# Sliding-window attention and gated feed-forward on one core: a reordered opening, six V buffers, rotating PSUM banks, last tiles in four banks

## The chip, the core and the metric

The kernel runs on one NeuronCore of a Trainium2 chip. The metric is the device time of one execution in microseconds (us). TensorE is called PE below, its weight load PEld, VectorE DVE, ScalarE ACT, GpSimd POOL, SyncE SP.

## The reference

Eight batches, eight heads, 576 positions, head size 64. Each position attends to itself and the 63 before it. The result, 4608 tokens of 512 numbers, goes through a gated feed-forward layer of width 1536.

```python
scores = q @ k.T / sqrt(64); mask = (rel >= 0) & (rel < 64)
x = softmax(scores, mask) @ v                  # then (4608, 512)
out = (silu(x @ w_gate) * (x @ w_val)) @ w_out # w: 512x1536, 512x1536, 1536x512
```

## The kernel before

Tokens are cut into 36 *chunks* of 128 and 9 *blocks* of 512 (four chunks). For each chunk `n` there are four steps on PE, each ended by copies on DVE or ACT: `T(n)` transposes K and Q, `Sx(n, half)` makes scores, `AV(n, half)` multiplies by V, and `X(n)` transposes the result into `xT`, the input of the feed-forward layer. For each block `c` there are 12 *feature slices* `F(c, f)`, two groups of four matmuls and then tanh on ACT and two DVE operations, and four *output tiles* `O(c, u)` of 12 matmuls. While block `c` is computed, the attention of the next four chunks is interleaved. PE writes its results into eight *banks* of a buffer named PSUM, from which DVE and ACT copy them; by the recorded order a bank is written again only when it has been emptied.

Each operation is recorded with the tiles that it reads and writes; each engine then runs its operations in the recorded order, and waits follow from reads and writes. Loads are issued by POOL, in the recorded order as well, and convert f32 to bf16 on the way. The window of a chunk reaches into the chunk before, so V is needed a second time, shifted by 64 rows: `vb[n]` holds the upper half of chunk `n-1` and the lower half of chunk `n`, copied within the core by DMAs that SP issues.

```python
NQ = 4; NV = 4; NZ = 3                          # buffers of q/k, v, transposed q
self.gb = ps[0:4]; self.ob = ps[4]; self.ab = ps[5:8]   # PSUM banks: F, O, attention

def load(self, n, which):
    ...                                         # POOL: q, k or v of chunk n, by HBM segments
    if which == "v":
        hi = [("va", i, 0), ("va", i, 1), ("va", i)]
        g.op("sp", ... dma_start(vb[64:128], va[0:64]), reads=hi, writes=[("vb", i, 1)], dma=True)
        if n + 1 < NCH:
            i2 = (n + 1) % self.NV              # n = 3: i2 = 0, the buffer of chunk 0
            g.op("sp", ... dma_start(vb2[0:64], va[64:128]), reads=hi, writes=[("vb", i2, 0)], dma=True)

def build(self):
    ...                                         # loads of chunks 0 to 3, weight slices 0 to 3
    self.T(0); self.Sx(0, 0); self.T(1); self.Sx(0, 1)
    for n in range(0, 4):
        self.AV(n, 0)
        self.Sx(n + 1, 0) if n < 3 else None
        self.AV(n, 1)
        self.Sx(n + 1, 1) if n < 3 else None
        self.X(n)
        if n < 2: self.T(n + 2)
    for w in late_w: self.load_w(*w)            # slices 4 to 11, 512 columns a piece
    more(4)                                     # q, k, v of chunk 4
    self.load_wo(0, 6); self.load_wo(6, 12)     # w_out
    more(5)                                     # q, k, v of chunk 5
    self.T(4); self.F(0, 0); self.Sx(4, 0); self.Sx(4, 1)
    for c in range(NFC):
        for u in range(4):
            n = 4 * c + u + 4
            more(n + 2)
            ...                                 # F(c, 3u); AV(n, 0); [T(5) if n == 4]; Sx(n+1, 0)
            ...                                 # F(c, 3u+1); AV(n, 1); Sx(n+1, 1); O(c-1, u)
            ...                                 # X(n); F(c, 3u+2); T(n+2)
    for u in range(4): self.O(NFC - 1, u)       # the last four tiles, all in bank 4
```

The softmax here doesn't subtract the row's maximum and nothing guards it: scores larger than these inputs give would overflow.

## Time and profile before

| | before |
|---|---|
| time, median of 4 runs | 404.03 us |
| span of the profiled run | 403.1 us |
| first AV | 23.5 us |
| first feature slice | 40.2 us |
| second block starts | 85.97 us |
| last four output tiles start | 386.58 us |

The page cuts the span into 40 slices of about 10 us. A digit is the busy share in tenths; PEclk is the granted PE clock, DMA the mean busy share of the 16 DMA engines.

```profile
PE   1156498789999999999999999999999999999975
PEclk9999879989999999999999999999999999999999
DMA  9999996667777888787887777777777310010012
```

PE is full from the tenth slice on. Before that it is not, and for the first six slices the DMA engines are full instead: the loss lies in the opening, and at the very end.

The windows view gives busy us (and instructions) of PE, PEld, DVE, ACT and POOL in a stretch, then granted clock, DMA share (the summed time of the packets over that of 16 engines, which can pass 1) and GB/s. The third line is the steady part, from the second block to the last tiles; the fourth is the end.

```profile
40.00:50.00 10.00, 4.32 (x36) 2.59 (x36) 4.36 (x10) 2.90 (x6) 1.75 (x2) 0.90 1.91 183
50.00:60.00 10.00, 9.41 (x62) 4.97 (x62) 5.63 (x12) 3.79 (x7) 2.62 (x3) 0.76 1.69 154
...
85.97:386.58 300.61, 296.33 (x2099) 159.12 (x2137) 209.47 (x441) 121.46 (x209) 65.83 (x79) 1.00 0.60 73
386.58:403.10 16.52, 10.83 (x47) 4.37 (x48) 0.00 (x0) 2.39 (x4) 0.00 (x0) 1.00 0.16 63
```

The steady part is 98.6% PE (296.33 of 300.61 us), so nothing but the first 86 us and the last 16.5 us can give much. The chain that ended last (start, length, what) shows where the opening waits:

```profile
12.84 10.66 issue
23.50 0.22 PE ps L355
...
29.16 18.28 DMA kn<-in_k_dram
```

Two large pieces stand there: 10.66 us of "issue", which means that the profile shows no releaser, ahead of the first AV (L355), and a DMA of 18.28 us, the K of chunk 5, ahead of `T(5)` (L307). The timeline (start, length, engine, line, operation, count, and in brackets the idle time before it) tells more about each:

```profile
18.12 0.60 SPq L283 DMA_DIRECT2D vb<-va  x1
...
40.19 1.31 PE L399 MATMUL ps<-xT,Wg 128*128 128x512 bf16 x3 [0.22 <-issue]
47.49 0.40 PE L307 MATMUL ps<-ident,kn 128*128 128x128 bf16 x4 [3.10 <-DMA kn<-in_k_dram]
51.42 1.91 PE L399 MATMUL ps<-xT,Wv 128*128 128x512 bf16 x4
55.87 1.03 PE L399 MATMUL ps<-xT,Wv 128*128 128x512 bf16 x4
...
390.03 2.76 PE L421 MATMUL ps<-Wo,hT 128*128 128x512 bf16 x12 [0.69 <-ACT ost L426]
```

The first line is the copy of chunk 3's upper half into `vb[0]`. It is issued at 18.12 us, and copies of that kind landed about 5 us later, which is when the first AV starts. Chunk 0 does not need those rows, because its mask sets them to zero, but the buffer is the same and the copy was recorded first. Then `T(5)` waits for its K, after which four matmuls take 1.91 us where a full clock takes 1.03. The last line shows one bank shared by the last output tiles: PE waits for ACT to empty it.

### The profile page before, as it was taken

What the parts mean: (1) busy time and instruction counts of PE and PEld (TensorE: products, weight loads), DVE (VectorE), ACT (ScalarE), POOL (GpSimd) and SP (SyncE); (2) the same over time, 40 slices, a digit from 0 to 9 for tenths busy, and PEclk for the clock granted to TensorE, in tenths of its full rate; (3) what the DMA queues carried; (4) which work ended last, traced back from release to release, by engine and by line L of the source; (5) the groups of instructions that cost most, each with busy time, mean ns of one, the idle gap of its engine ahead of it and who ended that gap; (6) DMA issues with size and microseconds to landing.
All of it is one profiled execution on the core that took longest, in us unless ns stands there. A gap on an engine that the chain in (4) does not pass through costs nothing.

```text
span 403.1 us, 6537 instructions
## 1 busy us (share of the span) xinstructions
PE 355.7 (88%) x2546; PEld 194.7 (48%) x2592; DVE 255.1 (63%) x558; ACT 148.0 (37%) x254; POOL 111.2 (28%) x140
## 2 busy tenths in 40 slices
PE   1156498789999999999999999999999999999975
PEld 1045244445555555555555555555555555544432
DVE  4136467767777767667777776777777777655510
ACT  2122334334444444444444444444444444233211
POOL 8986122324333322233222222233222000000000
PEclk9999879989999999999999999999999999999999
DMA  9999996667777888787887777777777310010012
GB/s 78 179 210 192 181 148 56 57 48 83 83 82 85 87 86 88 85 90 84 97 98 96 90 85 83 82 84 83 81 83 83 56 36 26 28 52 28 26 52 78
DMA packets 130253, 34.54 MB, mean 86 GB/s; under 512 B 116464, under 2 KB 125616, under 8 KB 130224
## 3 DMA queue, kind: packets, MB, share of 16 engines
q0 software_dynamic: 119360, 18.88, 63.0%
q1 hardware_dynamic: 10864, 15.26, 10.8%
q8 instruction: 20, 0.33, 0.3%
q14 instruction: 9, 0.07, 0.1%
HBM read 37.75 MB, written 9.44 MB: 117 GB/s over the span
## 4 chain that ended last, share of the span: by engine, by line
PE 79%; DMA 6%; DVE 6%; issue 5%; ACT 3%; POOL 2%; POOLq 0%; DVEq 0%
PE ps L399 42%; PE ps L421 23%; DMA kn<-in_k_dram 6%; PE ps L329 5%; PE ps L307 3%; DVE uu L407 2%; PE ps L377 2%; DVE hT L409 2%; PE ps L355 2%; PE ps L356 2%; ACT sig L405 1%; ACT qz L313 1%; DVE xb L365 1%; ACT ost L426 1%; POOL va L274 1%
## 5 line engine op out<-in xcount | busy, mean ns | idle before, releaser
L407 DVE SCALAR_TENSOR_TENSOR uu<-sig,ps 128x512 bf16<-128x512 bf16 x108 | 74.1, 686 | 72.4 <-ACT sig L405 72.4
L399 PE MATMUL ps<-xT,Wv 128*128 128x512 bf16 x432 | 112.6, 384 | 0.0
L399 PE MATMUL ps<-xT,Wg 128*128 128x512 bf16 x407 | 107.7, 385 | 1.6 <-issue 0.4
L421 PE MATMUL ps<-Wo,hT 128*128 128x512 bf16 x411 | 96.4, 379 | 4.6 <-ACT ost L426 2.3
L274 POOL DMA_DIRECT2D va<-in_v_dram x40 | 33.7, 844 | 199.0 <-PE ps L356 171.0
L405 ACT ACTIVATE sig<-ps 128x512 bf16<-128x512 f32 x108 | 63.9, 592 | 45.4 <-PE ps L399 45.4
L409 DVE SCALAR_TENSOR_TENSOR hT<-uu,ps 128x512 bf16<-128x512 bf16 x108 | 74.2, 687 | 4.6 <-PE ps L399 0.9
L399 PEld LDWEIGHTS ps<-xT,Wv 128*128 128x128 bf16 x432 | 42.8, 99 | 52.4 <-issue 2.5
L421 PEld LDWEIGHTS ps<-Wo,hT 128*128 128x128 bf16 x432 | 40.7, 98 | 48.7 <-ACT ost L426 3.5
L337 ACT ACTIVATE pt<-ps 128x512 bf16<-128x512 f32 x72 | 42.9, 597 | 49.5 <-PE ps L329 47.1
L399 PEld LDWEIGHTS ps<-xT,Wg 128*128 128x128 bf16 x432 | 38.8, 99 | 29.5 <-issue 1.6
L426 ACT ACTIVATE ost<-ps 128x512 f32<-128x512 f32 x36 | 21.5, 597 | 81.2 <-PE ps L421 81.2
L313 ACT ACTIVATE qz<-ps 64x512 bf16<-64x512 bf16 x36 | 21.3, 591 | 75.4 <-DVE kT L312 75.4
L355 PE MATMUL ps<-vb,pt 128*128 128x65 bf16 x288 | 28.9, 200 | 13.4 <-issue 12.3
L274 POOL DMA_DIRECT2D qn<-in_q_dram x40 | 34.4, 866 | 2.3 <-PE ps L307 1.4
L355 PEld LDWEIGHTS ps<-vb,pt 128*128 128x128 bf16 x288 | 24.4, 103 | 21.4 <-issue 12.8
L274 POOL DMA_DIRECT2D kn<-in_k_dram x40 | 34.6, 873 | 0.0
L329 PE MATMUL ps<-qz,kT 128*128 128x128 bf16 x288 | 30.1, 231 | 5.0 <-ACT qz L313 2.5
L343 DVE TENSOR_TENSOR pt<-pt,mask 128x512 bf16<-128x512 bf16 x72 | 29.9, 417 | 6.2 <-ACT pt L337 6.2
L365 DVE TENSOR_TENSOR xb<-ps,rc 128x256 bf16<-128x256 f32 x72 | 30.6, 425 | 2.5
L383 DVE COPY xT<-ps 128x512 bf16<-128x512 bf16 x36 | 15.3, 424 | 24.6 <-PE ps L377 24.6
L356 PE MATMUL ps<-va,pt 128*128 128x65 bf16 x288 | 28.9, 200 | 0.0
(33 smaller groups left out, 179.1 us busy)
## 6 DMA issues: line engine op xcount, KB each, us to landing
out_dram<-ost SPq DMA_DIRECT2D x36, 256.0 KB, 3.3
vb<-va SPq DMA_DIRECT2D x71, 80.0 KB, 3.2
qn<-in_q_dram POOLq DMA_DIRECT2D x32, 128.0 KB, 4.5
kn<-in_k_dram POOLq DMA_DIRECT2D x32, 128.0 KB, 4.6
va<-in_v_dram POOLq DMA_DIRECT2D x32, 128.0 KB, 3.5
Wo<-in_moe_w_out_dram POOLq DMA_DIRECT2D x2, 768.0 KB, 16.6
Wg<-in_moe_w_gate_dram POOLq DMA_DIRECT2D x2, 512.0 KB, 10.8
Wv<-in_moe_w_val_dram POOLq DMA_DIRECT2D x2, 512.0 KB, 12.6
```

Source lines behind the costliest of these rows:

```text
L274: g.op("pool", lambda e, d=d, a=a: e.dma_start(d, a), writes=ks, dma=True)
L329: r = e.matmul(sv[:, w, c], self.kT[:, pr, k0:k0 + 128], qz[:, pr, :, 64 * w:64 * w + 64], start=True, stop=True)
L337: g.op("act", lambda e: e.activation(po, si, ACTF.Exp, scale=SCALE), reads=[bk], writes=[pk])
L343: g.op("dve", lambda e: e.tensor_tensor(po, po, m, ALU.mult), reads=[pk, "mask"], writes=[pk])
L355: e.matmul(av[:, j, :], pt[:, h, 0:128], vb[:, h, 0:65], start=True, stop=False)
L356: r = e.matmul(av[:, j, :], pt[:, h, 64:192], va[:, h, 0:65], start=False, stop=True)
L365: g.op("dve", lambda e: e.tensor_tensor(xo, av[:, :, 0:64], rb, ALU.mult), reads=[bk, ("rc", ir)], writes=[("xb", ix, half)])
L399: r = e.matmul(bank[:, :], W[:, kk, f * 128:f * 128 + 128], xT[:, kk, :], start=(kk == 0), stop=(kk == NK - 1))
L405: g.op("act", lambda e: e.activation(sig[:, :], G[:, :], ACTF.Tanh, scale=0.5), reads=[gk], writes=[("sig", i)])
L407: g.op("dve", lambda e: e.scalar_tensor_tensor(uu[:, :], sig[:, :], 1.0, G[:, :], ALU.add, ALU.mult), reads=[("sig", i), gk], writes=[("uu ...
L409: g.op("dve", lambda e: e.scalar_tensor_tensor(hT[:, f, :], uu[:, :], 0.5, V[:, :], ALU.mult, ALU.mult), reads=[("uu", i), vk], writes=[(" ...
L421: r = e.matmul(OB[:, :], hT[:, f, 128 * u:128 * u + 128], self.Wo[:, f, :], start=(f == 0), stop=(f == NF - 1))
```

## The change

The intent: let chunks 0 to 3 overlap over all eight banks, let feature slices start as soon as their weights land, take weight slices in feature order between chunk loads, and put the last tiles in four banks. NV becomes 6, which takes chunk 3's copy out of chunk 0's buffer, and NZ becomes 4. The `lo` and `hi` lines let each V copy wait only for the segment that it reads. Cut to its core:

```diff
-    NV = 4
-    NZ = 3
+    NV = 6
+    NZ = 4
...
+        self.rot = {"f": ([0, 1, 2, 3], 0), "o": ([4], 0), "a": ([5, 6, 7], 0)}
...
-        hi = [("va", i, 0), ("va", i, 1), ("va", i)]
+        lo = [("va", i, 0), ("va", i)]
+        hi = [("va", i, 0 if len(parts) == 1 else 1), ("va", i)]
...                       # build(): loads q,k,v of 0, 1, 2, then v,q,k of 3, slices 0 and 1
+        self.banks("a", [5, 6, 7, 4, 0, 1, 2, 3])
+        self.T(0); self.T(1); self.S(0); self.T(2); self.S(1); self.A(0); self.T(3); self.S(2)
+        self.A(1); self.X(0, "act"); self.S(3); self.A(2); self.X(1, "act"); self.A(3)
+        self.X(2, "act"); self.X(3, "act")          # (one call a line in the original)
+        self.banks("a", [5, 6, 7])
+        self.load_qk(4); W(2, 4); self.load_v(4); self.load_qk(5); W(4, 6); self.load_v(5)
+        self.load_qk(6); W(6, 8); self.load_v(6); self.load_qk(7); W(8, 10); self.load_v(7)
+        W(10, 12)
+        ...                                         # F(0,0) to F(0,3) between T(4), T(5), S(4)
+        self.load_wo(0, 6)
+        self.load_wo(6, 12)
+        nf = [2, 2, 2, 1]
+        for u in range(4):
+            n = 4 + u
+            if n + 4 < NCH:
+                self.load_qk(n + 4)                 # chunk 8 and on: issued after w_out
+                self.load_v(n + 4)
+            self.F(0, fi)
+            self.AV(n, 0)
+            self.Sx(n + 1, 0)
+            if nf[u] == 2:
+                self.F(0, fi + 1)
+            fi += nf[u]
+            self.AV(n, 1)
+            self.Sx(n + 1, 1)
+            self.T(n + 2)
+            if u == 3:
+                self.F(0, 11)
+            self.X(n)
...                                                 # blocks 1 to 8 as before; loads 4 chunks ahead
+        self.banks("o", [0, 1, 2, 3])
         for u in range(4):
             self.O(NFC - 1, u)
```

More of the change, by code (lines that the diff above doesn't have):

```diff
@@ L195, in alloc, with bank, banks, segs @@
         self.wup = sb("wup", 1, F32)
-        ps = [nc.alloc_psum_tensor("ps%d" % i, [128, 512], F32) for i in range(8)]
-        self.gb = ps[0:4]
-        self.ob = ps[4]
-        self.ab = ps[5:8]
-        self.n_gb = 0
-        self.n_ab = 0
-        self.n_s = 0
-    def gbank(self):
-        i = self.n_gb % 4
-        self.n_gb += 1
-        return self.gb[i], ("gb", i)
-    def abank(self):
-        i = self.n_ab % 3
-        self.n_ab += 1
-        return self.ab[i], ("ab", i)
-    def segs(self, n):
-        t0 = 128 * n
+        self.ps = [nc.alloc_psum_tensor("ps%d" % i, [128, 512], F32) for i in range(8)]
+        self.rot = {"f": ([0, 1, 2, 3], 0), "o": ([4], 0), "a": ([5, 6, 7], 0)}
+        self.n_s = 0
+    def bank(self, kind):
+        ids, i = self.rot[kind]
+        self.rot[kind] = (ids, i + 1)
+        j = ids[i % len(ids)]
+        return self.ps[j], ("ps", j)
+    def banks(self, kind, ids):
+        self.rot[kind] = (ids, 0)
+    def segs(self, t0, size):
         r = 0
-        while r < 128:
+        while r < size:
             b, s = divmod(t0 + r, S)
-            L = min(128 - r, S - s)
+            L = min(size - r, S - s)
             yield r, b, s, L
@@ L258, in init_pool_b, with load_qk @@
         self.g.op("pool", lambda e: e.memset(m[0:64, 128:192], 0.0), writes=["mask"])
-    def load(self, n, which):
-        g = self.g
-        if which == "v":
-            i = n % self.NV
-            dst, key, src = self.va[i], ("va", i), self.v
-        else:
-            i = n % self.NQ
-            dst, src = (self.qn[i], self.q) if which == "q" else (self.kn[i], self.k)
-            key = (which + "n", i)
-        parts = list(self.segs(n))
+    def load_qk(self, n):
+        i = n % self.NQ
+        for dst, src, nm in ((self.qn[i], self.q, "qn"), (self.kn[i], self.k, "kn")):
+            parts = list(self.segs(128 * n, 128))
+            for j, (r, b, s, L) in enumerate(parts):
+                d = dst[r:r + L]
+                a = src[b, :, s:s + L, :].rearrange("h p d -> p h d")
+                ks = [(nm, i, j)] if len(parts) > 1 else [(nm, i, 0), (nm, i, 1)]
+                self.g.op("pool", lambda e, d=d, a=a: e.dma_start(d, a), writes=ks, dma=True)
@@ L270, in load, with load_v @@
+    def load_v(self, n):
+        g = self.g
+        i = n % self.NV
+        va = self.va[i]
+        parts = list(self.segs(128 * n, 128))
         for j, (r, b, s, L) in enumerate(parts):
-            d = dst[r:r + L, :, 0:64]
-            a = src[b, :, s:s + L, :].rearrange("h p d -> p h d")
-            ks = [key + (j,)] if len(parts) > 1 else [key + (0,), key + (1,)]
+            d = va[r:r + L, :, 0:64]
+            a = self.v[b, :, s:s + L, :].rearrange("h p d -> p h d")
+            ks = [("va", i, j)] if len(parts) > 1 else [("va", i, 0), ("va", i, 1)]
@@ L274, in load @@
             g.op("pool", lambda e, d=d, a=a: e.dma_start(d, a), writes=ks, dma=True)
-        if which == "v":
-            vb = self.vb[i]
-            va = self.va[i]
-            hi = [("va", i, 0), ("va", i, 1), ("va", i)]
-            g.op("sp", lambda e: e.dma_start(vb[64:128], va[0:64]), reads=hi, writes=[("vb", i, 1)], dma=True)
-            if n + 1 < NCH:
-                i2 = (n + 1) % self.NV
-                vb2 = self.vb[i2]
-                g.op("sp", lambda e: e.dma_start(vb2[0:64], va[64:128]), reads=hi, writes=[("vb", i2, 0)], dma=True)
+        vb = self.vb[i]
@@ L285, in load_w @@
+        lo = [("va", i, 0), ("va", i)]
+        hi = [("va", i, 0 if len(parts) == 1 else 1), ("va", i)]
+        g.op("sp", lambda e: e.dma_start(vb[64:128], va[0:64]), reads=lo, writes=[("vb", i, 1)], dma=True)
+        if n + 1 < NCH:
+            i2 = (n + 1) % self.NV
+            vb2 = self.vb[i2]
+            g.op("sp", lambda e: e.dma_start(vb2[0:64], va[64:128]), reads=hi, writes=[("vb", i2, 0)], dma=True)
     def load_w(self, which, a, b):
@@ L299, in T @@
         qn, kn, qz = self.qn[iq], self.kn[iq], self.qz[iz]
-        bank, bk = self.abank()
+        bank, bk = self.bank("a")
         tb = bank[:, :].bitcast(BF).rearrange("p (w c t) -> p w c t", w=2, c=4)
@@ L320, in Sx @@
         qz, pt = self.qz[iz], self.pt[ip]
-        bank, bk = self.abank()
+        bank, bk = self.bank("a")
         sv = bank[:, :].rearrange("p (w c e q) -> p w c e q", w=2, c=2, e=2)
@@ L348, in AV @@
         va, vb, pt = self.va[iv], self.vb[iv], self.pt[ip]
-        bank, bk = self.abank()
+        bank, bk = self.bank("a")
         av = bank[:, 0:260].rearrange("p (h x) -> p h x", h=4)
@@ L366, in AV, with X @@
              reads=[bk, ("rc", ir)], writes=[("xb", ix, half)])
-    def X(self, n):
+    def X(self, n, eng="dve"):
         g = self.g
@@ L371, in X @@
         xb = self.xb[ix]
-        bank, bk = self.abank()
+        bank, bk = self.bank("a")
         tb = bank[:, 0:256].bitcast(BF).rearrange("p (c t) -> p c t", c=4)
@@ L382, in X @@
         xo = self.xT[it][:, :, 128 * u:128 * u + 128]
-        g.op("dve", lambda e: e.tensor_copy(xo, tb), reads=[bk], writes=[("xT", it, u)])
+        if eng == "dve":
+            g.op("dve", lambda e: e.tensor_copy(xo, tb), reads=[bk], writes=[("xT", it, u)])
+        else:
+            g.op("act", lambda e: e.activation(xo, tb, ACTF.Copy), reads=[bk], writes=[("xT", it, u)])
     def F(self, c, f):
@@ L392, in F @@
         xk = [("xT", it, u) for u in range(4)]
-        G, gk = self.gbank()
-        V, vk = self.gbank()
+        G, gk = self.bank("f")
+        V, vk = self.bank("f")
         def mm(bank, W):
@@ L416, in O @@
         io = (4 * c + u) % self.NO
-        ost, OB = self.ost[io], self.ob
+        ost = self.ost[io]
+        OB, ok = self.bank("o")
         def pe(e):
@@ L423, in pe @@
             return r
-        g.op("pe", pe, reads=[("hT", ih, f) for f in range(NF)] + [("Wo", f) for f in range(NF)], writes=["ob"])
-        g.op("act", lambda e: e.activation(ost[:, :], OB[:, :], ACTF.Copy), reads=["ob"], writes=[("ost", io)])
+        g.op("pe", pe, reads=[("hT", ih, f) for f in range(NF)] + [("Wo", f) for f in range(NF)], writes=[ok])
+        g.op("act", lambda e: e.activation(ost[:, :], OB[:, :], ACTF.Copy), reads=[ok], writes=[("ost", io)])
         r0 = 512 * c + 128 * u
@@ L428, in O, with S, A @@
         g.op("sp", lambda e: e.dma_start(self.out[r0:r0 + 128, :], ost[:, :]), reads=[("ost", io)], dma=True)
+    def S(self, n):
+        self.Sx(n, 0)
+        self.Sx(n, 1)
+    def A(self, n):
+        self.AV(n, 0)
+        self.AV(n, 1)
     def build(self):
+        W = lambda a, b: (self.load_w("g", a, b), self.load_w("v", a, b))
         self.init()
-        self.load(0, "q")
-        self.load(0, "k")
+        self.load_qk(0)
         self.init_pool_a()
-        self.load(0, "v")
-        self.load(1, "q")
@@ L437, in build @@
-        self.load(1, "k")
+        self.load_v(0)
+        self.load_qk(1)
         self.init_pool_b()
-        self.load(1, "v")
-        for n in (2, 3):
-            for w in "qkv":
-                self.load(n, w)
-        wl = [("g", 0, 1), ("v", 0, 1), ("g", 1, 2), ("v", 1, 2), ("g", 2, 4), ("v", 2, 4)]
-        for w in wl:
-            self.load_w(*w)
-        loaded = 4
-        def more(n):
-            nonlocal loaded
-            while loaded <= min(n, NCH - 1):
-                for w in "qkv":
-                    self.load(loaded, w)
-                loaded += 1
+        self.load_v(1)
@@ L455, in build @@
+        self.load_qk(2)
+        self.load_v(2)
+        self.load_v(3)
+        self.load_qk(3)
+        W(0, 1)
+        W(1, 2)
+        self.banks("a", [5, 6, 7, 4, 0, 1, 2, 3])
         self.T(0)
-        self.Sx(0, 0)
         self.T(1)
-        self.Sx(0, 1)
-        for n in range(0, 4):
-            self.AV(n, 0)
-            self.Sx(n + 1, 0) if n < 3 else None
-            self.AV(n, 1)
-            self.Sx(n + 1, 1) if n < 3 else None
-            self.X(n)
-            if n < 2:
-                self.T(n + 2)
@@ L467, in build @@
-        late_w = [("g", 4, 8), ("v", 4, 8), ("g", 8, 12), ("v", 8, 12)]
-        for w in late_w:
-            self.load_w(*w)
-        more(4)
+        self.S(0)
+        self.T(2)
+        self.S(1)
+        self.A(0)
+        self.T(3)
+        self.S(2)
+        self.A(1)
+        self.X(0, "act")
+        self.S(3)
+        self.A(2)
+        self.X(1, "act")
+        self.A(3)
+        self.X(2, "act")
+        self.X(3, "act")
+        self.banks("a", [5, 6, 7])
+        self.load_qk(4)
@@ L471, in build @@
+        W(2, 4)
+        self.load_v(4)
+        self.load_qk(5)
+        W(4, 6)
+        self.load_v(5)
+        self.load_qk(6)
+        W(6, 8)
+        self.load_v(6)
+        self.load_qk(7)
+        W(8, 10)
+        self.load_v(7)
+        W(10, 12)
+        self.F(0, 0)
+        self.F(0, 1)
+        self.T(4)
+        self.F(0, 2)
+        self.Sx(4, 0)
+        self.T(5)
+        self.F(0, 3)
+        self.Sx(4, 1)
         self.load_wo(0, 6)
         self.load_wo(6, 12)
-        more(5)
@@ L474, in build @@
-        self.T(4)
-        self.F(0, 0)
-        self.Sx(4, 0)
-        self.Sx(4, 1)
-        first = True
-        for c in range(NFC):
+        fi = 4
+        nf = [2, 2, 2, 1]
[5 more added lines that the diff above has]
+            self.F(0, fi)
+            self.AV(n, 0)
+            self.Sx(n + 1, 0)
+            if nf[u] == 2:
+                self.F(0, fi + 1)
+            fi += nf[u]
+            self.AV(n, 1)
+            self.Sx(n + 1, 1)
[3 more added lines that the diff above has]
+            self.X(n)
@@ L480, in build @@
+        for c in range(1, NFC):
             for u in range(4):
@@ L482, in build @@
                 live = n < NCH
-                more(n + 2)
-                if not first:
-                    self.F(c, 3 * u)
-                first = False
+                if n + 4 < NCH:
+                    self.load_qk(n + 4)
+                    self.load_v(n + 4)
+                self.F(c, 3 * u)
                 if live:
@@ L489, in build @@
                     if n + 1 < NCH:
-                        if n == 4:
-                            self.T(5)
                         self.Sx(n + 1, 0)
@@ L497, in build @@
                         self.Sx(n + 1, 1)
-                if c > 0:
-                    self.O(c - 1, u)
+                self.O(c - 1, u)
                 if live:
```

## The prediction

> **What bounds it now.** By the windows view TensorE is busy 197.9 of 200 us from 120 to 320 us and 59.5 of 60 from 320 to 380: PE-bound, and left alone by the change. The loss is in the opening. The second feed-forward block starts at 85.97 us (timeline), while the PE work before it is about 37 us at full clock (estimate: 12 feature slices of 1.73 us, 8 chunks of about 2 us, from matmul starts).
>
> Three losses:
> 1. The chain of waits shows 10.7 us of "issue" from 12.8 us to the first attention-times-V (AV) at 23.5. By the code it is a false dependency: with four V buffers, the copy of chunk 3's upper half overwrites chunk 0's shifted buffer, and the first AV, recorded later, waits for it. The copy was issued at 18.12 us; landing about 5 us later gives 23.4.
> 2. The first feature slice starts at 40.2 us; chunks 0 to 3 run nearly serially.
> 3. PE waits to 47.5 us for K of chunk 5 (18.3 us of DMA in the chain), queued behind w_out. Then the granted clock is 0.76 (50 to 60 us) and four matmuls take 1.91 us instead of 1.03; the Trainium skill, "TensorE: Matmul & The Clock Gate", Part 1, says idleness throttles the array, and this agrees.
>
> The DMA engines are saturated from about 3 to 54 us (the page's slices).
>
> **What changes.** Six V buffers remove the false wait: first AV at about 14 us. Eight banks and staggering let chunks 0 to 3 finish soon after chunk 3's data land (17.5 to 20.5 us): first feature slice at about 24 to 25 us. Weight slices then alternate with chunk loads and run as they land. Bytes hardly change; added are four ACT copies (0.6 us each) and about 1 us of memsets.
>
> **New bound.** The DMA queue. PE's order has chunk 8's transpose before feature slices 10 and 11, and chunk 8's Q and K are issued after w_out. The Trainium skill ("DMA: Bandwidth & Descriptors", "Two DMAs through the same engine are not ordered") says descriptors of one queue start in order, which the landings here agree with. Before, about 7.1 MB landed between 17.5 and 53.6 us: 196 GB/s. Now 7.5 MB must land before that transpose: 17.5 + 38.3 = about 56 us (estimate). After it come two slices, AV of chunk 7, scores of 8, two transposes: 6.2 us warm, but partly cold clock and the last ACT-DVE chain: 9 to 10 us. The second block starts at about 66 us instead of 86: 20 us, all critical.
>
> **Tail.** The last four output tiles share one bank; PE waits 0.69, 0.69 and 0.92 us for the eviction (timeline). Four banks remove about 2.2 us.
>
> **Steady part.** Earlier loads and more buffers: under 1 us; only 2.1 us in 200 were idle.
>
> **Sum.** 404.3 - 20 - 2.2 = about 382 us; range 375 to 390.
>
> **What the profile would show.** Right: no 10 us "issue" piece; first feature slice at 24 to 27 us; DMA full to about 56 us; the longest PE wait on K or Q of chunk 8, ending at 54 to 58 us; second block at 64 to 68 us; PE near 99% afterwards; the last 48 matmuls back to back. Wrong: second block before 62 us (the queue runs faster, or chunk 8 doesn't gate) or after 70 (256-column slices transfer slower, or V copies or the cold clock delay every slice).
>
> **What would make it wrong.** DMA rate with smaller weight slices; queue order unlike issue order; half clock through the fragmented stretch; ACT's copies delaying exponentials.
>
> Chances: faster 0.97, within 2% 0.025, slower 0.005.

## The result

Ratios here are the mean time of one kernel's fast runs over that of the other's fast runs of the same rounds, so not quite the ratio of the medians quoted beside them.

| | before | after |
|---|---|---|
| time, median of 4 runs | 404.03 us (403.75 to 404.44) | 384.42 us (383.22 to 386.57) |
| ratio | | 0.952 (95%: 0.9476 to 0.9563) |
| first AV | 23.5 us | 15.3 us |
| first feature slice | 40.2 us | 27.05 us |
| second block starts | 85.97 us | 68.34 us |
| second block to last tiles | 300.6 us | 300.4 us |
| last four tiles to the end | 16.5 us | 14.0 us |

The three stretches add up to the 20.4 us that the profiled spans differ by: 17.6 in the opening, 0.2 in the steady part, 2.55 at the end. The page's slices after:

```profile
PE   1579758899999999999999999999999999999986
PEclk9999997999999999999999999999999999999999
DMA  9999999978777777878777787877771000010002
```

PE is full from the ninth slice on (about 77 us instead of 91), and the DMA engines are full for eight slices instead of six (about 77 us instead of 60). The windows of the same two stretches, of the steady part and of the end:

```profile
40.00:50.00 10.00, 7.59 (x73) 4.77 (x76) 9.17 (x22) 4.49 (x8) 7.44 (x10) 1.00 1.43 210
50.00:60.00 10.00, 5.85 (x50) 3.68 (x50) 5.64 (x13) 2.66 (x5) 2.15 (x3) 0.81 1.93 176
...
68.34:368.73 300.39, 296.15 (x2096) 159.03 (x2134) 208.22 (x438) 121.00 (x208) 61.16 (x73) 1.00 0.61 73
368.73:382.70 13.97, 10.48 (x47) 4.61 (x48) 0.00 (x0) 2.39 (x4) 0.00 (x0) 1.00 0.19 75
```

From 40 to 50 us it is now DVE that is nearly full (9.17 us of 10), and from 50 to 60 us PE again has a hole. The chain of waits names it:

```profile
38.04 18.97 DMA kn<-in_k_dram
...
66.32 0.70 DVE uu L408
67.04 0.69 DVE hT L410
67.73 0.34 DVE xT L382
```

The K of chunk 8, 18.97 us from issue to landing, now ends the last wait of the opening. Behind it, the second block's first matmul waits for the DVE work of feature slice 11 and only then for the copy of chunk 7's transpose. In the timeline:

```profile
27.05 0.81 PE L400 MATMUL ps<-xT,Wg 128*128 128x512 bf16 x3 [0.92 <-ACT xT L384]
57.10 0.59 PE L305 MATMUL ps<-ident,kn 128*128 128x128 bf16 x4 [3.93 <-DMA kn<-in_k_dram]
60.04 1.91 PE L400 MATMUL ps<-xT,Wv 128*128 128x512 bf16 x4
68.34 0.81 PE L400 MATMUL ps<-xT,Wg 128*128 128x512 bf16 x3 [2.20 <-DVE xT L382]
...
368.73 10.53 PE L423 MATMUL ps<-Wo,hT 128*128 128x512 bf16 x47 [1.27 <-DVE hT L410]
```

The last line replaces four groups with waits between them: the last tiles run back to back. (One of the 48 matmuls has no record.)

### The profile page after: what moved, and what is told of

It reads as the page before. It is cut to its first block, busy times and chain, and to the rows that moved or that the text cites. A ratio compares the mean times of both kernels' runs of the same rounds, so it can differ in the third digit from the quotient of the medians.

```text
span 382.7 us, 6546 instructions
## 1 busy us (share of the span) xinstructions
PE 350.6 (92%) x2546; PEld 193.3 (50%) x2592; DVE 253.8 (66%) x558; ACT 149.6 (39%) x258; POOL 114.3 (30%) x144
## 4 chain that ended last, share of the span: by engine, by line
PE 81%; POOL 8%; DMA 5%; issue 2%; DVE 2%; ACT 1%; POOLq 0%
PE ps L400 43%; PE ps L423 24%; DMA kn<-in_k_dram 5%; PE ps L327 5%; PE ps L305 3%; POOL va L273 2%; PE ps L354 2%; PE ps L353 2%; POOL qn L262 2%; PE ps L375 2%; POOL kn L262 2%; POOL Wv L287 1%; POOL Wg L287 1%; DVE uu L408 1%; ACT sig L406 1%
## 5 line engine op out<-in xcount | busy, mean ns | idle before, releaser
L400 PE MATMUL ps<-xT,Wg 128*128 128x512 bf16 x408 | 106.4, 381 | 4.4 <-DVE xT L382 2.2
L262 POOL DMA_DIRECT2D qn<-in_q_dram x40 | 35.7, 897 | 168.4 <-PE ps L305 167.6
L273 POOL DMA_DIRECT2D va<-in_v_dram x40 | 36.4, 921 | 0.0
L262 POOL DMA_DIRECT2D kn<-in_k_dram x40 | 36.0, 907 | 0.0
L305 PE MATMUL ps<-ident,kn 128*128 128x128 bf16 x144 | 15.0, 231 | 16.3 <-DMA kn<-in_k_dram 16.3
L382 DVE COPY xT<-ps 128x512 bf16<-128x512 bf16 x32 | 13.6, 424 | 22.7 <-PE ps L375 22.6
L353 PE MATMUL ps<-vb,pt 128*128 128x65 bf16 x288 | 28.0, 198 | 0.0
L354 PE MATMUL ps<-va,pt 128*128 128x65 bf16 x288 | 27.9, 198 | 0.0
## 6 DMA issues: line engine op xcount, KB each, us to landing
Wo<-in_moe_w_out_dram POOLq DMA_DIRECT2D x2, 768.0 KB, 17.6
```

Of the source, the lines that this page charges most:

```text
L262: self.g.op("pool", lambda e, d=d, a=a: e.dma_start(d, a), writes=ks, dma=True)
L273: g.op("pool", lambda e, d=d, a=a: e.dma_start(d, a), writes=ks, dma=True)
L353: e.matmul(av[:, j, :], pt[:, h, 0:128], vb[:, h, 0:65], start=True, stop=False)
L354: r = e.matmul(av[:, j, :], pt[:, h, 64:192], va[:, h, 0:65], start=False, stop=True)
L400: r = e.matmul(bank[:, :], W[:, kk, f * 128:f * 128 + 128], xT[:, kk, :], start=(kk == 0), stop=(kk == NK - 1))
```

## The experiments

My theory was that the opening is bound by the one queue in which POOL's loads stand, that the order in that queue is most of the gain, and that the false wait of the first AV and the banks matter little by themselves. The rivals were that the false wait, the staggering, or the total of bytes made the difference. Twelve kernels ran. Eleven gave the right result; one did not.

### Six V buffers alone

```diff
-    NV = 4
+    NV = 6          # kernel before, nothing else
```

> The kernel before with six V buffers and nothing else: only the false wait of the first AV goes. My theory (the opening is bound by the DMA queue, this wait hides under it): first AV moves from 23.5 to about 13 us and the first feature slice from 40.2 to about 36 to 37 us (then it waits for K of chunk 4), but the wait for K of chunk 5 still ends at about 47 us, so the time stays 404 us, within 1.5 us. Rival (the 10.7 us in the chain of waits were really lost): about 394 us.

Measured: 405.31 us beside 404.78 us for the kernel before, ratio 1.0002 (0.9983 to 1.0021). Its PE timeline:

```profile
12.42 0.24 PE L355 MATMUL ps<-vb,pt 128*128 128x65 bf16 x1 [0.27 <-DVE pt L343]
36.66 0.60 PE L307 MATMUL ps<-ident,kn 128*128 128x128 bf16 x4 [9.78 <-DMA kn<-in_k_dram]
47.34 0.61 PE L307 MATMUL ps<-ident,kn 128*128 128x128 bf16 x4 [4.22 <-DMA kn<-in_k_dram]
```

This shows two things. The 10.66 us of "issue" was the false dependency: with the buffer taken apart the first AV starts at 12.42 us. And it was worth nothing: the time won is spent waiting for K of chunk 4 (9.78 us) and of chunk 5, which lands at 47 us as ever. A piece in the chain of waits is not a saving; what matters is when the next thing on the path is ready.

### The last tiles in four banks, alone

```diff
-        ost, OB = self.ost[io], self.ob
+        ost = self.ost[io]
+        OB, ok = (self.gb[u], ("gb", u)) if last else (self.ob, "ob")   # last: final loop only
```

> The kernel before with only the last four output tiles in four banks: their matmuls run back to back and the time falls by 2.0 to 2.6 us, to about 401.7 us; the rest of the trace stays as it was. Rival (the rest of the tail waits on stores): no gain.

Measured: 401.90 us beside 404.78, ratio 0.9926 (0.9905 to 0.9946), so 3.0 us. In the trace the last four tiles start at 385.89 us and the span ends at 399.9: 14.0 us, where the kernel before takes 16.5. The trace gives 2.5 us and the interval of the times holds that. This part stands by itself.

### The order of the loads, with the old computation

```diff
-    NV = 4
+    NV = 6
...      # kernel before: chunk 3 as v, q, k, then slices 0 and 1, and before T(4):
+        for n in (4, 5, 6, 7):
+            self.load(n, "q")
+            self.load(n, "k")
+            W(2 * n - 6, 2 * n - 4)
+            self.load(n, "v")
+        W(10, 12)
+        self.load_wo(0, 6)
+        self.load_wo(6, 12)
...      # and in the loop, in place of more(n + 2): q, k, v of chunk n + 4
```

> The kernel before with its order of computation and its banks, but six V buffers and the loads in the order of the changed kernel. Theory that the order of the loads is the main gain: the wait for K of chunk 5 at 47 us goes, slices start at about 30 us, the steps of about 9 us run from there, the second block starts at 67 to 70 us and the time is 386 to 391 us. Rival (staggering over all banks is the main gain): at least 395 us.

Measured: 389.45 us beside 404.78, ratio 0.9613 (0.9588 to 0.9638). The computation stands in its old order, in three banks.

```profile
28.11 1.49 PE L399 MATMUL ps<-xT,Wg 128*128 128x512 bf16 x3 [0.22 <-issue]
47.92 0.40 PE L377 MATMUL ps<-ident,xb 128*128 128x128 bf16 x4 [1.81 <-DVE xb L365]
56.96 0.54 PE L377 MATMUL ps<-ident,xb 128*128 128x128 bf16 x4 [1.81 <-DVE xb L365]
69.66 1.03 PE L399 MATMUL ps<-xT,Wg 128*128 128x512 bf16 x4
```

The second block starts at 69.66 us (last line), so 16.3 of the 17.6 us of the opening come with the loads and the V buffers. After the first few us no PE wait is on a DMA any more. The steps are 9.04 us long (47.92 to 56.96), and what PE waits for in each is DVE. In times, 404.78 x (1 - 0.9613) = 15.7 us for the loads and 404.78 x (1 - 0.9926) = 3.0 us for the tiles leave about 1 us of the whole change (404.78 x (1 - 0.952) = 19.4 us) for the banks, the staggering, NZ and the ACT copies together. The interval of each of these ratios is 0.8 to 1.8 us wide on either side, so this rest is not told from zero.

### Three banks in the opening of the changed kernel

```diff
-        self.banks("a", [5, 6, 7, 4, 0, 1, 2, 3])
+        self.banks("a", [5, 6, 7])
```

> The changed kernel with the three banks of before in the opening, all else kept. Theory (DMA queue binds until chunk 8's K lands at 57 us): the first slice moves from 27 us to 28 to 31 us, the wait for chunk 8's K still ends at about 57 us, the second block starts at 68 us, time 384 to 386 us. Rival (eight banks matter): 388 us or more.

Measured: 384.88 us, ratio 0.9486 (0.9459 to 0.9512).

```profile
29.62 1.91 PE L400 MATMUL ps<-xT,Wv 128*128 128x512 bf16 x4
57.27 0.38 PE L305 MATMUL ps<-ident,kn 128*128 128x128 bf16 x4 [0.45 <-issue]
67.12 0.81 PE L400 MATMUL ps<-xT,Wg 128*128 128x512 bf16 x3 [2.20 <-DVE xT L382]
```

The first slice moves to 28.34 us, the K of chunk 8 lands at about the same time as ever (38.05 us plus 19.1 us), and the second block starts at 67.12 us. The banks are worth nothing here: what they win sits in front of the wait for chunk 8. Its transpose started at 57.27 us after an idle time of 0.45 us instead of 3.93. Not all of that is due to the banks: in this run the first slices also ran at half rate (1.91 us for four matmuls, first line), although the windows view gives a granted clock of 1.00 there. That time was lost in the same place, and cost as little.

### w_out behind chunks 8 and 9

```diff
-        self.load_wo(0, 6)
-        self.load_wo(6, 12)
...
+            if u == 1:                # after the loads of chunk 9
+                self.load_wo(0, 6)
+                self.load_wo(6, 12)
             self.F(0, fi)
```

> The changed kernel with w_out issued behind the loads of chunks 8 and 9 instead of ahead of them; bytes and computation the same. Theory (chunk 8's K is late only because w_out is ahead of it in the queue): its K lands near 49 to 50 us, before the slices in front of its transpose are done (53 us), so the 3.9 us wait and the cold clock after it go; the second block starts at 62 to 64.5 us and the time is 379 to 381 us. Rival (the opening is bound by total bytes, whatever their order, or the first output tile then waits for w_out): 383.5 us or more.

Measured: 381.71 us beside 405.24, ratio 0.9424 (0.9403 to 0.9445). The K of chunk 8 was issued at 36.5 us and took 13.0 us, so it landed at 49.5 us as expected, and no step of the opening waits for a load after chunk 3. But the slices in front of its transpose were done at 55.3 us, not at 53, and the second block started at 65.76 us, not at 62 to 64.5:

```profile
55.30 0.39 PE L305 MATMUL ps<-ident,kn 128*128 128x128 bf16 x4
60.77 0.40 PE L327 MATMUL ps<-qz,kT 128*128 128x128 bf16 x4 [1.11 <-DVE xb L363]
65.76 0.81 PE L400 MATMUL ps<-xT,Wg 128*128 128x512 bf16 x3 [2.19 <-DVE xT L382]
```

The cause that the theory names is confirmed, since moving w_out alone moves the landing by 7.5 us. The size was too large for two reasons that the trace shows. In this run the granted clock was 0.72 from 20 to 30 us, which makes the first slices late. And DVE is busy 9.29 us of 10 from 40 to 50 us, so the path runs through DVE and ACT as soon as the load is out of it. The limit of the queue lay only about 3 us beyond that second one (68.34 to 65.76 us is 2.6 us; the ratios, from different calls, give nearly 4).

### Chunk 8's transpose after the last slices

```diff
             self.AV(n, 0)
-            self.Sx(n + 1, 0)
+            if u < 3:
+                self.Sx(n + 1, 0)
...                                    # the same for Sx(n + 1, 1); T(n + 2) only for u < 2
+        self.T(8)
+        self.S(8)
+        self.T(9)
```

> The changed kernel with its loads untouched; TensorE does chunk 8's transpose and scores and chunk 9's transpose after slices 10 and 11 and chunk 7. Theory (it is the place of that transpose in TensorE's order that turns late bytes into idle time): no wait over 1 us on chunk 8's K, second block at 61 to 64 us, 378 to 381 us. Rival (slices 10 and 11 would have waited anyway, for weights or for VectorE): 383.5 us or more.

Measured: 381.58 us, ratio 0.9417 (0.9402 to 0.9433).

```profile
63.71 0.61 PE L327 MATMUL ps<-qz,kT 128*128 128x128 bf16 x8 [1.85 <-ACT qz L311]
64.81 0.81 PE L400 MATMUL ps<-xT,Wg 128*128 128x512 bf16 x3
```

The K landed at 57.4 us and nobody waited for it; the second block started at 64.81 us. So the late K costs nothing where PE has other work in front of it. The second block again came later than expected: the transpose at 61.25 us was followed by a wait of 1.85 us for its own copies, and, as in the run before, the first slices had a low clock (0.70 from 20 to 30 us).

### Chunk 7's output transpose ahead of slice 11

```diff
+            self.X(n)
             if u == 3:
                 self.F(0, 11)
-            self.X(n)
```

> The changed kernel with chunk 7's output transpose ahead of feature slice 11, whose VectorE chain it now waits behind. Theory: the 2.2 us wait of the second block's first matmul for that copy goes and 1.3 to 2.2 us are won: 382.2 to 383.2 us. Rival (VectorE's backlog only shows elsewhere): within 0.7 us of the changed kernel.

Measured: 381.63 us, ratio 0.942 (0.9399 to 0.9442), a little more than expected.

```profile
57.53 0.38 PE L305 MATMUL ps<-ident,kn 128*128 128x128 bf16 x4 [2.49 <-DMA kn<-in_k_dram]
66.02 1.03 PE L400 MATMUL ps<-xT,Wg 128*128 128x512 bf16 x4
```

The 2.20 us wait of the second block for DVE is gone; that block started at 66.02 us, 8.49 us after chunk 8's transpose at 57.53, where the changed kernel takes 11.24 us (57.10 to 68.34). This is a cost of the change's own order that the prediction did not see.

### Four V buffers in the changed kernel

```diff
-    NV = 6
+    NV = 4          # changed kernel
```

> The changed kernel with four V buffers again, so the false wait of the first AV is back. Theory (there is slack of about 4 us in front of chunk 8's K, and the opening is fed by DMA): first AV at about 21 us, first slice at 31 to 33 us, the wait for chunk 8's K shrinks to under 1 us, and the time is 384 to 388 us. Rival (without the extra buffers the change is lost): over 392 us.

A failed experiment: 407.9 us and a wrong result (relative error 1.32). The changed order records the load of chunk `n + 4` before `AV(n)`. With four buffers both use the same one, so `AV(4)` reads chunk 8's V, and waits for it:

```profile
62.96 0.24 PE L353 MATMUL ps<-vb,pt 128*128 128x65 bf16 x1 [19.00 <-DMA vb<-va]
```

This says nothing of the theory or of the rival, only that the six buffers are part of the new load order and can't be taken out of it. The next experiment asks the question properly.

### The false wait put back, and nothing else

```diff
         av = bank[:, 0:260].rearrange("p (h x) -> p h x", h=4)
+        extra = [("vb", 4, 0)] if n == 0 else []      # chunk 3's copy
...
-        ... ("vb", iv, 0), ("vb", iv, 1)], writes=[bk])
+        ... ("vb", iv, 0), ("vb", iv, 1)] + extra, writes=[bk])
```

> The changed kernel with the false wait alone put back, by a dependency that no data needs: the first AV also waits for the copy of chunk 3's upper V half. Theory (slack ahead of chunk 8's K hides it): first AV from about 16 to 21 us, first slice from 27 to 29 to 32 us, K of chunk 8 still at about 57 us with a shorter wait, time within 1.5 us of the changed kernel run beside it. Rival (the false wait costs its length): 4 us or more slower than the changed kernel.

Measured: 385.89 us, ratio 0.9536 (0.9516 to 0.9555); the changed kernel beside it, below, 384.69 us and 0.9516. The first AV starts at 21.70 us and the first slice at 31.67:

```profile
21.70 0.21 PE L354 MATMUL ps<-vb,pt 128*128 128x65 bf16 x1 [6.25 <-issue]
```

6.25 us more of waiting there cost about 1 us in the end, and as the two intervals overlap, even that is not told from zero. The second block started at 69.63 us. The slack in front of chunk 8's K took most of it, as the theory has it, and the profile calls this wait "issue" again, although its cause was put in by hand.

### The changed kernel once more

```diff
 # no edit
```

> The changed kernel once more, unchanged, beside the other runs of this call: 383.5 to 385.5 us; it says how far the single steps (381.6 to 381.7) are really below it and how much its first slices and its wait for chunk 8's K vary from run to run.

Measured: 384.69 us (383.44 to 386.34, 5 runs), ratio 0.9516 (0.9491 to 0.9541). Its second block started at 68.52 us, and K of chunk 8 ended the wait at 57.27. So the single steps above, with ratios of about 0.942, lie about 1% below the changed kernel. They ran on another chip, and each is compared through the kernel before.

### The best combination tried

w_out behind chunk 9, chunk 7's output transpose ahead of slice 11, and the copies of chunks 4 to 7 on ACT:

```diff
...                                    # w_out as above
+            self.X(n, "act")
             if u == 3:
                 self.F(0, 11)
-            self.X(n)
```

> w_out behind chunks 8 and 9, chunk 7's output transpose ahead of slice 11, and in addition the copies of the output transposes of chunks 4 to 7 on ScalarE instead of VectorE (4 times 0.42 us of VectorE work less). Theory (once chunk 8's K is no longer awaited, VectorE's chain of about 9.2 of 10 us sets the pace): the second block starts at 61.5 to 64 us, 377.5 to 380 us, below each single step (381.6 to 381.7). Rival (the single steps remove the same 3 us and something else binds): 381 us or more.

Measured: 380.90 us (379.80 to 381.07), ratio 0.9412 (0.9396 to 0.9428), in the same call as the 0.9516 of the changed kernel: 1.1% below it (0.9412 / 0.9516 = 0.989). It beats both kernels. The second block started at 64.83 us, and the time fell between what the theory and the rival expected. DVE fell to 8.57 and 7.44 us of 10:

```profile
40.00:50.00 10.00, 8.21 (x83) 4.96 (x81) 8.57 (x21) 5.02 (x9) 5.42 (x7) 1.00 1.87 187
50.00:60.00 10.00, 7.52 (x74) 4.63 (x77) 7.44 (x19) 5.02 (x10) 5.27 (x6) 1.00 1.39 215
```

The chain of waits of this run alternates between ACT and DVE from 32 to 62 us; the copy of the output transpose now stands in ACT's line ahead of a tanh. The single steps do not add up: the combination's 0.9412 is inside the interval of each of them. That fits a path out of which each step takes a piece, while another path of nearly the same length runs beside it; it is argued from the chain and was not tested. How much of the 1.1% each part gives was not separated.

### Wider weight slices

```diff
-        W(4, 6)
+        W(4, 8)                       # 512 columns a piece
...
-        W(6, 8)
...
-        W(8, 10)
+        W(8, 12)
...
-        W(10, 12)
```

> The changed kernel with slices 4 to 11 of the two input weights loaded in 512-column pieces (as before the change) instead of 256-column ones; same bytes, two pairs of loads instead of four. It tests the 1.1 us by which chunk 8's K came later (57.1 us) than predicted (56). Theory (narrower pieces transfer slower): K of chunk 8 is awaited only to 55.8 to 56.4 us and the time is 0.5 to 1.5 us below the changed kernel. Rival (the width does not matter and the byte estimate was short): 56.8 us or later, time within 0.7 us of the changed kernel.

Measured: 384.90 us, ratio 0.952 (0.9503 to 0.9536). The K of chunk 8 was issued at 35.17 us and took 21.4 us, so it landed at about 56.6 us, between the two expectations. In the seven runs with narrow slices and w_out ahead of that K it landed at 56.7 to 57.4 us (issue plus time to landing, one profile each), so at most 0.8 us can be the width, and it may be nothing. The time did not move. In the changed kernel's trace 7.63 MB moved between 17.5 and 57 us at 193 GB/s; the prediction had 7.5 MB at 196, so both factors were a little off.

## Why the prediction was right

It said 382 us, range 375 to 390; the median was 384.42. The direction, the size and the main mechanism held. Point by point:

- **The false wait of the first AV.** Right as a cause: with six buffers alone the first AV moved to 12.4 us, and with the whole change to 15.3, where about 14 was predicted. The prediction counted it as one of three "losses"; alone it was worth 0.0% before the change and, put back, about 1 us or nothing after it.
- **The first feature slice at 24 to 25 us.** It came at 27.05. This had no effect: three banks moved it to 28.3 at the same time.
- **The new bound is the DMA queue, through chunk 8's K behind w_out.** Right. The estimate was 56 us and the wait ended at 57.1. Moving w_out moved the landing to 49.5 us; moving the transpose took the wait away. The Trainium skill, "DMA: Bandwidth & Descriptors", section "SWDGE vs HWDGE vs iDMA", says that only one queue is allocated for DMAs issued from GpSimd, and the section that the prediction cites says that "Within one queue of one SDMA engine, descriptors *start* in order". The trace agrees: the profile lists one such queue, and the landing followed w_out by its place in it.
- **9 to 10 us from there to the second block.** This term was mis-sized: 11.24 us. Of it 2.20 us was the wait for chunk 7's copy behind slice 11's DVE work, which the seventh run removed (8.49 us). The cold clock, which the prediction had in this term, explains part of the rest: in the three-bank run, with the same 2.20 us wait but groups of four matmuls at 1.03 us throughout, the stretch took 9.85 us (57.27 to 67.12). Together with the 1.1 us by which the K came later than 56, this term is why the second block started at 68.34 us, just outside the predicted 64 to 68, and why the opening gave 17.6 us instead of 20.
- **The tail, 2.2 us.** The trace shows 2.55 us, and the tail alone 2.5.
- **The steady part, under 1 us.** 0.2 us.
- **The clock.** The Trainium skill, "TensorE: Matmul & The Clock Gate", Part 1, has a half clock after an idle window of about 3.4 us. The 3.93 us wait here was followed by matmul groups at 1.91 us instead of 1.03, and 0.81 was granted from 50 to 60 us. The prediction counted on a "partly cold clock" and got one.
- **DMA full to about 56 us.** A miss without effect: the DMA engines stayed full to about 72 us, on loads of later chunks, and no PE wait in the rest of the opening is on one of them.
- **What was not foreseen.** A second limit close behind the first. DVE and ACT need almost as long for the opening as the queue does, so removing the queue's last wait starts the second block 2.6 us sooner, not the wait's 3.9 us plus the cold clock.

What stays open: which part of the new load order (chunks ahead of w_out, narrower weight pieces, earlier issue) gives how much of the gain, since only the whole order was put into the old kernel; the share of the slice width in the late landing; and why the first slices ran at half clock in some runs and not in others. The changed kernel and the runs with w_out, the transpose of chunk 8 or that of chunk 7 moved have the same code up to the fourth slice, yet the two profiles of the first had a clock of 1.00 from 20 to 30 us and the other three 0.70 to 0.72.

## What to carry to other kernels

Where all loads stand in one queue, the order in the queue is a schedule of its own: give each load the place that its first consumer has in PE's order, and keep a large tensor that is needed late behind small ones that are needed soon. Before valuing a wait in the chain, find when the next thing on the path will be ready; a wait of 10.7 us can be worth nothing, and is best tested by removing it alone. When one limit goes, look at once for the second one, here the DVE and ACT work of the same stretch, for it caps what is left to win.

## What the Trainium skill lacked or had wrong

- "TensorE: Matmul & The Clock Gate", Part 1, ties the half clock to an idle window of about 3.4 us. Here it also came without such a gap. In the combination run no PE wait between 19 and 30 us is over 1.1 us, yet groups of four matmuls of its first two slices took 1.91 us and 0.78 was granted from 20 to 30 us. In two profiles of the changed kernel, with nearly the same waits, the clock stayed at 1.00 and they took 1.03. In the run with chunk 7's output transpose moved, three matmuls took 1.49 us instead of 0.81 right after a wait of 2.49 us. The page's "A second HAM failure mode: psum-queue depth-cycling" describes short idle times between groups that set the clock swinging, which would fit; it gives no gap length, and none can be read off here either.
- "DMA: Bandwidth & Descriptors", Bandwidth, gives 341 GB/s for a 1 MB load from HBM issued by GpSimd, but no figure for loads that convert f32 to bf16 in short rows. Here, with the queue full, Q, K and V moved at 156 GB/s of bf16 written (from 46 to 50 us before the change), and the stretch with w_out in it at 207 (from 37 to 40 us).
- The same page's cost of about 2.0 us plus bytes over 436 GB/s ("Anatomy of one DMA") is for one DMA by itself. For planning an opening the wait in the queue counts: the 128 KB of chunk 8's K took 18.97 us from issue to landing.
